# A recurrent attention kernel with a routed feed-forward: another order in the first step and in the tail

## The chip, the cores and the metric

The kernel runs on one core of one Trainium2 chip. The metric is the device time of one execution in microseconds (us). Three executions of the kernel before took 1936.31, 1943.81 and 1943.49 us: the median is 1943.49 us.

## The reference

Two blocks read the same normalised rows `xn` of x (2048 rows of 1024, bf16), and their results are added to x.

```
xn = layernorm(x)
# A: 64 segments of 32 rows, one after the other; mem is 8 rows of 1024
for s in range(64):
    h = concat(mem, xn[32*s : 32*s+32])              # 40 rows
    q, k, v = h @ Wq, h @ Wk, h @ Wv                 # 1024 -> 32 heads x 128
    p = softmax(mask(q k^T * scale))
    o = (p v) @ Wo                                   # 4096 -> 1024
    mem = o[:8]
    out_A[32*s : 32*s+32] = o[8:]
# B: the two rows with the largest xn @ w_r go through a feed-forward of 3584
y = (silu(x_sel @ w_gate) * (x_sel @ w_up)) @ w_down * sigmoid(r_sel)
result = x + out_A + (xn with y added at the two rows)
```

`mem` makes block A a chain of 64 steps. A step's stationary operand holds 32 columns: the 8 memory rows and 24 of the segment's 32 rows. The other 8 rows of each segment, here called the left rows, don't depend on `mem`, and their q, k and v are made for all 64 segments at once in the first step; their attention is done in each step, and their product with Wo again for all segments after the last one.

## The kernel before

**Tiling.** The four weight matrices are cut into 64 granules of 512 KB: granules 0 to 47 are the q, k and v weights in the six phases `PHASES` (q and k of the first half of the heads, q and k of the second half, v of the first half, v of the second half, eight granules each), granules 48 to 63 are Wo. Most stay in SBUF (`resident`). Eighteen (`streamed`) don't fit and are loaded again in each of the 64 steps, from a packed copy `wsc` in DRAM, through five slots (`wstream`). `fetch` issues the next streamed load on SyncE (SP) whenever `after` or `left_done` reports that one has been used. SP issues in program order, so a load that waits for a slot holds all SP loads behind it.

**Step s.** For each phase TensorE multiplies the step's 32 stationary columns by eight granules into PSUM (line 678); hooks between granules do the transposes, scores, softmax (`scores`, `exponent`, `soften`) and `attend`. Then 16 Wo granules are multiplied (`project`, line 712), the result becomes the rows of the output and the memory rows of the next step. `attend` places its sums in PSUM: in the tile WO of pool `psA`, which has two buffers, and in `OPB` for the first half of the heads, in `BS` and `OPB` for the second.

**The first step** does more. It loads all weights, takes the statistics of all 16 tiles of 128 rows (`row_stats`), runs the router (`spread`, `router_tile`, `router_out`, `router_top`), and projects the left rows of all segments: `left_qk` makes 16 heads of q or k, each a chain of eight matmuls into a `psA` buffer and a copy by ScalarE, and stores them to `ql_d` on GpSimd's queue; `left_v` makes 16 blocks of v in the same way, copied in turn by ScalarE and VectorE into four quarters of one SBUF tile VG and stored to `vl_d` on GpSimd's queue (line 496), each quarter being overwritten four blocks later. At the end of `left_v` the rows that step 0 itself needs are read back (tile VL, line 500). `left_done(p)` follows phase p: slots are refilled, and resident areas that served as scratch are loaded (W8B, eight granules, after phase 3; W2 and the last resident granule after phase 5). Before all that come `left_stats` and `left_turns`, which normalise and transpose the left rows.

**The tail** after step 63: `left_rows_out(k)`, k = 0 and 1, multiplies the attention output of the left rows (tile OTA, loaded back from `ol_d` in 16 pieces of 256 KB by `load_left_out`) with the 16 Wo granules (tile WD, line 786; 128 matmuls each), adds x and stores. `gate_up` multiplies the two selected rows by the feed-forward weights (GU, line 848), then come the activation and the product with w_down (YP, line 871). The feed-forward weights are 46 loads (`fetch_moe`), 16 of w_gate and 16 of w_up of 448 KB and 14 of w_down of 512 KB, each needing a home: 22 homes come free during the last step, the others as `gate_up` uses what it has. At the very end the two routed rows are read back from the output, added to and stored.

Of the kernel before, what the change touches and what calls it, by code (L numbers as in the profile page):

```python
# [9 lines left out]
F32 = mybir.dt.float32  # L10
# [18 lines left out]
def kernel(  # L29
# [186 lines left out]
    def left_rows():  # L216
        for t in range(4):
            nc.sync.dma_start(out=XLR[:, t, :], in_=x_left[t, :, XM:SEG, :])

# [208 lines left out]


    left_rows()  # L430
    load_x(0)
    nc.sync.dma_start(out=WRB, in_=B_w_r.unsqueeze(0).to_broadcast([P, D]))
# [24 lines left out]
    left_turns()  # L457
    for t in range(1, NT):
        row_stats(xt(t), S6, MV[:, t, :])

    gathered = {}

    def left_qk(p, mat, half, Gs, between):
        if mat == 0:
            gathered[half] = area(f"big{half}", [P, NSEG, 256], "GA")
        GA = gathered[half].rearrange("p s (m i q r) -> p s m i q r", m=2, i=4, q=4)
        for h in range(16):
            PSG = psA.tile([P, 512], F32, tag="acc", name="PSG")
            for kc in range(KC):
                nc.tensor.matmul(PSG[:, :], lhsT=part(Gs[kc], h // 4)[:, P * (h % 4):P * (h % 4 + 1)], rhs=XLT[:, kc, :],  # L470
                                 start=(kc == 0), stop=(kc == KC - 1))
            nc.scalar.copy(out=GA[:, :, mat, h % 4, h // 4, :], in_=PSG.rearrange("p (s r) -> p s r", r=XL))
            if h % 2 == 1:
                next(between, None)
        for _ in between:
            pass
        if mat == 1:
            G3 = gathered[half]
            if half == 0:
                qkl[0] = one.tile([P, 2, 2, 4, 4, XL], BF16, tag="bA", name="QKL")  # L480
            nc.vector.tensor_copy(out=qkl[0][:, half].rearrange("p m i q r -> p (m i q r)"), in_=G3[:, 0, :])
            for k in range(NSEG // 4):
                nc.gpsimd.dma_start(out=ql_d[k // 2][half, 4 * (k % 2):4 * (k % 2) + 4].rearrange("s p c -> p s c"),
                                    in_=G3[:, 4 * k:4 * (k + 1), :])

    def left_v(half, Gs):
        VG = home(hm, [P, 2048], BF16, "VG")
        for b in range(4):
            for jq in range(4):
                PSV = psA.tile([P, 512], F32, tag="acc", name="PSV")  # L490
                for kc in range(KC):
                    nc.tensor.matmul(PSV[:, :], lhsT=XLT[:, kc, P * b:P * (b + 1)], rhs=part(Gs[kc], jq),  # L492
                                     start=(kc == 0), stop=(kc == KC - 1))
                VQ = VG[:, 512 * jq:512 * (jq + 1)]
                (nc.vector.tensor_copy if jq % 2 else nc.scalar.copy)(out=VQ, in_=PSV[:, :])
                nc.gpsimd.dma_start(out=vl_d[b][4 * jq:4 * jq + 4, :, :, half, :].rearrange("i s r e -> (s r) i e"),
                                    in_=VQ.rearrange("p (i e) -> p i e", i=4))
# [34 lines left out]
    def after(s, g):  # L532
# [17 lines left out]

    def load_left_out(k):
        nc.gpsimd.dma_start(out=areas["big0"][:, 4 * k:4 * k + 4, :], in_=ol_d[k // 4][4 * (k % 4):4 * (k % 4) + 4].rearrange("s p c -> p s c"))

    qkl = [None]
    group = {}

    for s in range(NSEG):
# [113 lines left out]
        for p, (mat, half) in enumerate(PHASES):  # L671
# [13 lines left out]
            if mat < 2:  # L685
# [4 lines left out]
                if s == 0:  # L690
                    left_qk(p, mat, half, [Gv_ for _, Gv_ in behind],
                            (x for g_, Gv_ in behind if g_ in KEPT_COLS for x in keep(g_, Gv_)))
            else:
# [25 lines left out]
        for w in range(16):  # L719
# [60 lines left out]
    def left_rows_out(k):  # L780
        WD = [[psK.tile([P, 512], F32, name=f"WD{2 * b + c}", tag=f"kept{2 * b + c}") for c in range(2)] for b in range(2)]
        for i, (g, Gv) in enumerate(WOS.items()):
            for hs in range(2):
                for b in range(2):
                    for c in range(2):
                        nc.tensor.matmul(WD[b][c][:, :], lhsT=OTR[:, P * (2 * k + b):P * (2 * k + b + 1), 2 * (g - 48) + hs],  # L786
                                         rhs=Gv[:, D * hs + 512 * c:D * hs + 512 * (c + 1)],
                                         start=(i + hs == 0), stop=(i == 15 and hs == 1))
        for b in range(2):
            x = left_x(2 * k + b)  # L790
# [50 lines left out]

    def gate_up(w):
        for kc in range(KC):
            for fh in range(2):
                Gt = moe_tiles["gu", w, kc, fh]
                for fl in range(FC // 2):
                    col = (w * FC + fh * (FC // 2) + fl) * 2
                    nc.tensor.matmul(GU[:, col:col + 2], lhsT=Gt[:, fl * P:(fl + 1) * P], rhs=XSELT[:, kc, :],
                                     start=(w + kc + fh + fl == 0), stop=True, skip_group_check=True)
                free_homes.append(moe_home["gu", w, kc, fh])  # L850
                fetch_moe()

    gate_up(0)
    left_rows_out(1)
    nc.vector.memset(ROW, 0.0)
    for c in range(2):
        nc.gpsimd.dma_start(out=quarters(c), in_=routed(vals[c]))
    gate_up(1)
    assert not moe
# [53 lines left out]
```

## Time and profile before

| | |
|---|---|
| median of three executions | 1943.49 us |
| profiled execution, time | 1954.35 us |
| profiled execution, span of the core | 1952.7 us |
| granted TensorE clock, mean | 0.972 |
| TensorE matmul busy | 1578.2 us (81%) |
| VectorE, ScalarE, GpSimd busy | 907.6, 767.1 and 359.2 us |
| moved by DMA | 672.39 MB, mean 344 GB/s |

A page and several views were taken from one profiled execution. The chain of waits follows the work that ended last back to the start. A timeline row has the start, the duration, the engine and line, output and input tiles, the count of merged instructions, and in brackets the idle time of the engine before them with what ended it. In a table of windows each engine has its busy time and count, then come the granted TensorE clock, the DMA engines' busy share and GB/s.

### The profile page before, as it was taken

What the parts mean: (1) busy time and instruction counts of PE and PEld (TensorE: products, weight loads), DVE (VectorE), ACT (ScalarE), POOL (GpSimd) and SP (SyncE); (2) the same over time, 40 slices, a digit from 0 to 9 for tenths busy, and PEclk for the clock granted to TensorE, in tenths of its full rate; (3) what the DMA queues carried; (4) which work ended last, traced back from release to release, by engine and by line L of the source; (5) the groups of instructions that cost most, each with busy time, mean ns of one, the idle gap of its engine ahead of it and who ended that gap; (6) DMA issues with size and microseconds to landing.
All of it is one profiled execution on the core that took longest, in us unless ns stands there. A gap on an engine that the chain in (4) does not pass through costs nothing.

```text
span 1952.7 us, 70934 instructions
## 1 busy us (share of the span) xinstructions
PE 1578.2 (81%) x30353; PEld 819.4 (42%) x30378; DVE 907.6 (46%) x2774; ACT 767.1 (39%) x2018; POOL 359.2 (18%) x635
## 2 busy tenths in 40 slices
PE   6997678888888888888887888888888888887677
PEld 3443234444444444444443444444444444444345
DVE  7711144555555555555454445545555554454230
ACT  2331134444444444444444444444444444444200
POOL 1224221111111111111111111111111111111300
PEclk9998999999999999999999999999999999999888
DMA  9688299999999999999999999999999999999984
GB/s 351 243 283 258 55 348 369 376 382 366 362 378 369 371 362 367 367 372 371 365 374 344 357 363 375 373 357 353 372 375 365 375 379 365 356 374 355 363 311 172
DMA packets 213853, 672.39 MB, mean 344 GB/s; under 512 B 31424, under 2 KB 34800, under 8 KB 213536
## 3 DMA queue, kind: packets, MB, share of 16 engines
q1 hardware_dynamic: 186896, 617.17, 84.2%
q0 software_dynamic: 25488, 48.58, 7.7%
q8 instruction: 237, 3.88, 0.7%
q10 hardware_dynamic: 1152, 2.10, 0.4%
q14 instruction: 80, 0.66, 0.1%
HBM read 646.74 MB, written 29.76 MB: 346 GB/s over the span
## 4 chain that ended last, share of the span: by engine, by line
DMA 58%; PE 32%; DVE 3%; ACT 3%; issue 2%; POOL 0%; ACTq 0%; SPq 0%; DVEq 0%; POOLq 0%
DMA g<-wsc 54%; PE PSm L678 11%; PE WO L712 7%; PE PSG L470 6%; PE PSV L492 3%; PE WD L786 2%; DMA MW<-in_B_w_gate_dram 1%; PE BT L568 1%; DMA XLS<-in_A_x_dram 1%; ACT OTL L648 1%; ACT OT L646 1%; PE BS L637 1%; DMA MW<-in_B_w_down_dram 0%; DVE BS L601 0%; ACT BS L605 0%
## 5 line engine op out<-in xcount | busy, mean ns | idle before, releaser
L678 PE MATMUL PSm<-wres,ST 128*32 128x512 bf16 x6400 | 539.6, 386 | 22.2 <-DVE ST L333 22.2
L678 PEld LDWEIGHTS <-ST 128*32 128x32 bf16 x12288 | 303.0, 96 | 508.5 <-issue 179.4
L678 PE MATMUL PSm<-g,ST 128*32 128x512 bf16 x3332 | 335.4, 388 | 157.7 <-DMA g<-wsc 153.4
L687 ACT CAST XB<-PSm 128x512 bf16<-128x512 f32 x256 | 150.2, 587 | 265.9 <-PE PSm L678 263.4
L712 PEld LDWEIGHTS <-OT 128*32 128x32 bf16 x8192 | 205.2, 97 | 72.4 <-issue 57.3
L544 POOL DMA_DIRECT2D QKL<-ql_d x63 | 46.9, 744 | 910.7 <-DVE OTL L648 902.7
L578 DVE COPY KT<-BT 128x512 bf16<-128x512 bf16 x128 | 53.1, 415 | 260.8 <-PE BT L568 258.3
L712 PE MATMUL WO<-W8B,OT 128*32 128x256 bf16 x4096 | 164.1, 278 | 0.0
L678 PE MATMUL PSm<-W8A,ST 128*32 128x512 bf16 x2048 | 159.3, 383 | 0.0
L712 PE MATMUL WO<-g,OT 128*32 128x256 bf16 x2560 | 133.1, 279 | 24.2 <-DMA g<-wsc 23.6
L744 POOL DMA_DIRECT2D out_dram<-XN x256 | 128.6, 513 | 84.3 <-DVE XN L742 67.9
L377 ACT COPY BK<-KEPT 128x512 bf16<-128x512 bf16 x126 | 78.3, 621 | 99.0 <-PE WO L712 99.0
L390 DVE COPY g<-KEPT 128x512 bf16<-128x512 bf16 x126 | 53.6, 425 | 134.5 <-PE PSm L678 126.3
L695 ACT CAST VM<-PSm 128x512 bf16<-128x512 f32 x128 | 80.0, 625 | 77.0 <-PE PSm L678 77.0
L573 ACT COPY QT<-BT 128x512 bf16<-128x512 bf16 x128 | 75.0, 586 | 86.1 <-PE BT L568 48.5
L568 PEld LDWEIGHTS <-XB 128*128 128x128 bf16 x1024 | 58.5, 98 | 109.0 <-ACT XB L687 41.5
L568 PE MATMUL BT<-IDENT,XB 128*128 128x128 bf16 x1024 | 102.6, 223 | 0.1
L470 PE MATMUL PSG<-XLT,wres 128*128 128x512 bf16 x324 | 98.7, 379 | 0.3
L595 DVE TENSOR_TENSOR BS<-BS,CT 128x96 f32<-128x96 f32 (+1 forms) x256 | 59.7, 233 | 83.9 <-PE BS L588 79.4
L610 DVE TENSOR_REDUCE DN<-BS 128x8 f32<-128x320 f32 x128 | 62.9, 492 | 67.9 <-ACT BS L605 67.9
L576 ACT COPY KT<-QKL 128x128 bf16<-128x128 bf16 x128 | 38.2, 298 | 138.7 <-PE BT L568 95.5
L294 POOL DMA_DIRECT2D XN<-in_A_x_dram x64 | 34.0, 530 | 301.7 <-PE PSm L678 257.9
(178 smaller groups left out, 2491.8 us busy)
## 6 DMA issues: line engine op xcount, KB each, us to landing
g<-wsc SPq DMA_DIRECT2D x950, 512.0 KB, 6.3
g<-wsc SPq DMA_DIRECT2D x126, 256.0 KB, 5.6
g<-wsc SPq DMA_DIRECT2D x63, 384.0 KB, 5.7
ql_d<-GA POOLq DMA_DIRECT2D x32, 256.0 KB, 6.5
QKL<-ql_d POOLq DMA_DIRECT2D x63, 128.0 KB, 5.5
MW<-in_B_w_gate_dram SPq DMA_DIRECT2D x16, 448.0 KB, 12.7
MW<-in_B_w_up_dram SPq DMA_DIRECT2D x16, 448.0 KB, 9.3
MW<-in_B_w_down_dram SPq DMA_DIRECT2D x14, 512.0 KB, 9.8
```

Of the source, the lines that this page charges most:

```text
L377: copy(out=back[c], in_=KEPT_COLS[KEPT_WHOLE][c])
L470: nc.tensor.matmul(PSG[:, :], lhsT=part(Gs[kc], h // 4)[:, P * (h % 4):P * (h % 4 + 1)], rhs=XLT[:, kc, :], start=(kc == 0), stop=(kc == K ...
L492: nc.tensor.matmul(PSV[:, :], lhsT=XLT[:, kc, P * b:P * (b + 1)], rhs=part(Gs[kc], jq), start=(kc == 0), stop=(kc == KC - 1))
L568: nc.tensor.transpose(out=PTq[:, il, :, :].rearrange("p j r -> p (j r)"), in_=XB[:, il * P:(il + 1) * P], identity=IDENT[:, :])
L573: nc.scalar.copy(out=QT[half][:, :, :], in_=pv)
L595: nc.vector.tensor_tensor(out=S4, in0=S4, in1=m, op=ALU.add)
L610: nc.vector.tensor_reduce(out=DN[:, :], in_=S8, axis=AX.X, op=ALU.add)
L678: nc.tensor.matmul(PSm[32 * jq:32 * jq + 32, :], lhsT=ST[:, kc, :], rhs=part(Gv, jq), start=(kc == 0), stop=(kc == KC - 1), tile_position= ...
L687: nc.scalar.copy(out=XB[:, :], in_=PSm[:, :])
L695: nc.scalar.copy(out=VM[half][:, :], in_=PSm[:, :])
L712: nc.tensor.matmul(PS[32 * g:32 * g + 32, 0:256], lhsT=lhs(h), rhs=Gv[:, D * hs + 256 * g:D * hs + 256 * (g + 1)], start=False, stop=(last ...
L744: nc.gpsimd.dma_start(out=out2[s * SEG:s * SEG + XM, 256 * g:256 * (g + 1)], in_=OB[32 * g:32 * g + XM, :])
```

## The change

In the first step:

- The left rows are loaded on two queues, and ahead of all else come the first column halves of the eight granules of phase 0 (alternately on SP's and ScalarE's queue); x and the second column halves follow.
- The left rows are normalised and transposed first, and `left_qk` makes eight of the 16 heads of phase 0 before `spread`, the normalisation of step 0's rows and the statistics of the other 15 tiles. The other eight heads come after phase 0 as before.
- `left_v` stores on SP's queue, and reads VL back after its second block row instead of after the last.
- W8B is loaded after phase 4 instead of phase 3.
- In step 0 `attend` puts the first half's sums into `BS`, and the `psA` buffer of WO is taken only after all six phases.

In the tail:

- During the last step's Wo product one feed-forward load is issued after each of the five streamed granules, instead of two after each granule.
- Of the 16 loads of OTA, eight are issued on GpSimd's queue in the last step and eight on SP's after the loop, instead of twelve and four on GpSimd's.
- `left_rows_out` finishes its first 128 rows before it begins the second.
- `gate_up` is cut at `early` pieces (22, as 46 loads less 22 homes are left) instead of after w_gate's 16.

```diff
 def left_rows():
     for t in range(4):
-        nc.sync.dma_start(out=XLR[:, t, :], in_=x_left[t, :, XM:SEG, :])
+        (nc.scalar if t % 2 else nc.sync).dma_start(out=XLR[:, t, :], in_=x_left[t, :, XM:SEG, :])
...
+first_phase = []
+def first_half(c):
+    for g, t in first_phase:
+        (nc.scalar if g % 2 and c == 0 else nc.sync).dma_start(
+            out=t[:, D * c:D * (c + 1)], in_=granule_dram(g)[:, D * c:D * (c + 1)])
 left_rows()
+for g in range(KC):
+    ...
+    first_phase.append((g, t))
+first_half(0)
 load_x(0)
...
-for g in range(32):
+first_half(1)
+nc.sync.dma_start(out=WRB, in_=B_w_r.unsqueeze(0).to_broadcast([P, D]))
+for g in range(KC, 32):
...
-left_stats()
-row_stats(xt(0), S6, MV[:, 0, :])
-spread(0, 1)
-norm_seg(0)
-ST = new_st(0)
-mem_to_st(OB, ST)
-left_turns()
-for t in range(1, NT):
-    row_stats(xt(t), S6, MV[:, t, :])
...
-def left_qk(p, mat, half, Gs, between):
+def left_qk(mat, half, Gs, between, h0=0, h1=16):
...
-            nc.gpsimd.dma_start(out=vl_d[b][4 * jq:4 * jq + 4, :, :, half, :].rearrange("i s r e -> (s r) i e"),
-                                in_=VQ.rearrange("p (i e) -> p i e", i=4))
-    if half == 0:
-        group["vl"] = one.tile([P, 2, P], BF16, tag="vl", name="VL")
-    nc.gpsimd.dma_start(out=group["vl"][:, half, :], in_=vl_d[0][:, 0, :, half, :])
+            nc.sync.dma_start(out=vl_d[b][4 * jq:4 * jq + 4, :, :, half, :].rearrange("i s r e -> (s r) i e"),
+                              in_=VQ.rearrange("p (i e) -> p i e", i=4))
+        if b == 1:
+            if half == 0:
+                group["vl"] = one.tile([P, 2, P], BF16, tag="vl", name="VL")
+            nc.sync.dma_start(out=group["vl"][:, half, :], in_=vl_d[0][:, 0, :, half, :])
 def left_done(p):
...
     elif p == 3:
         home_first()
+    elif p == 4:
         area("big1", [P, 8, 2048], "W8B")
         for g in AREAS["big1"]:
             load_resident(g)
 def after(s, g):
...
-        if g >= 47:
-            fetch_moe(2)
+        if g in streamed and g >= 48:
+            fetch_moe(1)
...
+left_stats()
+left_turns()
+row_stats(xt(0), S6, MV[:, 0, :])
+left_qk(0, 0, [t for _, t in first_phase], iter(()), 0, 8)
+spread(0, 1)
+norm_seg(0)
+ST = new_st(0)
+mem_to_st(OB, ST)
+for t in range(1, NT):
+    row_stats(xt(t), S6, MV[:, t, :])
 for s in range(NSEG):
...
-                nxt["wo"] = psA.tile([P, 512], F32, tag="acc", name="WO")
+                if s > 0:
+                    nxt["wo"] = psA.tile([P, 512], F32, tag="acc", name="WO")
...
-            sums[half] = [BS[:, 0:4 * NK] if half else nxt["wo"][:, 256:256 + 4 * NK], OPB]
+            sums[half] = [BS[:, 0:4 * NK] if half or s == 0 else nxt["wo"][:, 256:256 + 4 * NK], OPB]
...
     assert not hooks, hooks
+    if s == 0:
+        nxt["wo"] = psA.tile([P, 512], F32, tag="acc", name="WO")
...
         if w == 2 and s + 1 == NSEG:
-            for k in range(12):
-                load_left_out(k)
+            for k in range(8):
+                load_left_out(k, nc.gpsimd)
...
 fetch_moe()
-for k in range(12, 16):
-    load_left_out(k)
+for k in range(8, 16):
+    load_left_out(k, nc.sync)
...
 def left_rows_out(k):
-    for i, (g, Gv) in enumerate(WOS.items()):
-        for hs in range(2):
-            for b in range(2):
+    for b in range(2):
+        for i, (g, Gv) in enumerate(WOS.items()):
+            for hs in range(2):
                 for c in range(2):
                     nc.tensor.matmul(WD[b][c][:, :], ...)
-    for b in range(2):
         x = left_x(2 * k + b)
...
+pieces = [(w, kc, fh) for w in range(2) for kc in range(KC) for fh in range(2)]
+def gate_up(i0, i1):
+    for w, kc, fh in pieces[i0:i1]:
...
-gate_up(0)
+early = len(pieces) + FC // 2 - len(moe)
+gate_up(0, early)
 left_rows_out(1)
...
-gate_up(1)
+gate_up(early, len(pieces))
```

More of the change, by code (lines that the diff above doesn't have):

```diff
@@ L427, in granule @@
         return t
-    left_rows()
+    first_phase = []
[3 more added lines that the diff above has]
+                out=t[:, D * c:D * (c + 1)], in_=granule_dram(g)[:, D * c:D * (c + 1)])
+    left_rows()
+    for g in range(KC):
+        if g in first_streamed:
+            assert flow.pop(0) == (0, g)
+            t = wstream.tile([P, 2048], BF16, tag="g", name="g")
+            queued.append((g, t))
+        else:
+            t = res_tiles[g] = room(g, f"wres{g}")
+        first_phase.append((g, t))
+    first_half(0)
     load_x(0)
-    nc.sync.dma_start(out=WRB, in_=B_w_r.unsqueeze(0).to_broadcast([P, D]))
     load_seg(0)
@@ L449 @@
         load_resident(g)
[L451 to L459 removed]
     gathered = {}
[L463 to L464 removed]
+    def left_qk(mat, half, Gs, between, h0=0, h1=16):
+        if mat == 0 and h0 == 0:
             gathered[half] = area(f"big{half}", [P, NSEG, 256], "GA")
         GA = gathered[half].rearrange("p s (m i q r) -> p s m i q r", m=2, i=4, q=4)
[L467 removed]
+        for h in range(h0, h1):
             PSG = psA.tile([P, 512], F32, tag="acc", name="PSG")
@@ L549, in load_vl, with load_left_out @@
         nc.gpsimd.dma_start(out=group["vl"][:, :, :], in_=vl_d[s // 16][:, s % 16, :, :, :])
-    def load_left_out(k):
-        nc.gpsimd.dma_start(out=areas["big0"][:, 4 * k:4 * k + 4, :], in_=ol_d[k // 4][4 * (k % 4):4 * (k % 4) + 4].rearrange("s p c -> p s c"))
+    def load_left_out(k, queue):
+        queue.dma_start(out=areas["big0"][:, 4 * k:4 * k + 4, :], in_=ol_d[k // 4][4 * (k % 4):4 * (k % 4) + 4].rearrange("s p c -> p s c"))
     qkl = [None]
     group = {}
+    left_stats()
[8 more added lines that the diff above has]
+        row_stats(xt(t), S6, MV[:, t, :])
     for s in range(NSEG):
@@ L690 @@
                 if s == 0:
-                    left_qk(p, mat, half, [Gv_ for _, Gv_ in behind],
-                            (x for g_, Gv_ in behind if g_ in KEPT_COLS for x in keep(g_, Gv_)))
+                    left_qk(mat, half, [Gv_ for _, Gv_ in behind],
+                            (x for g_, Gv_ in behind if g_ in KEPT_COLS for x in keep(g_, Gv_)), 0 if p else 8)
             else:
@@ L840 @@
     GU = psA.tile([P, 512], F32, tag="acc", name="GU")
[L842 to L851, printed above, removed]
-    gate_up(0)
+    pieces = [(w, kc, fh) for w in range(2) for kc in range(KC) for fh in range(2)]
+    def gate_up(i0, i1):
+        for w, kc, fh in pieces[i0:i1]:
+            Gt = moe_tiles["gu", w, kc, fh]
+            for fl in range(FC // 2):
+                col = (w * FC + fh * (FC // 2) + fl) * 2
+                nc.tensor.matmul(GU[:, col:col + 2], lhsT=Gt[:, fl * P:(fl + 1) * P], rhs=XSELT[:, kc, :],
+                                 start=(w + kc + fh + fl == 0), stop=True, skip_group_check=True)
+            free_homes.append(moe_home["gu", w, kc, fh])
+            fetch_moe()
+    early = len(pieces) + FC // 2 - len(moe)
+    gate_up(0, early)
     left_rows_out(1)
```

## The prediction

> **What bounds the kernel now.** I read the table of windows over the three stages first, then the chain of waits.
>
> ```profile
> core 0: us, PE busy (x) PEld busy (x) DVE busy (x) ACT busy (x) POOL busy (x), PEclk, DMA share, GB/s
> 0.00:259.00 259.00, 204.35 (x1330) 95.52 (x1353) 95.57 (x213) 66.37 (x124) 68.57 (x113) 0.95 0.70 241
> 259.00:1829.00 1570.00, 1287.04 (x28056) 666.85 (x28044) 791.35 (x2505) 693.88 (x1878) 276.47 (x502) 0.99 0.99 368
> 1829.00:1952.00 123.00, 86.81 (x982) 57.02 (x981) 20.73 (x58) 6.83 (x16) 14.20 (x22) 0.79 0.74 265
> ```
>
> The middle, 1570 us, is the steps' weight stream: the DMA share is 0.99, and the change touches none of its transfers, so I carry it over unchanged. The ends are different: 0.30 x 259 = 78 us of the DMA engines stand unused in the first step and 0.26 x 123 = 32 us in the tail. What shortens those two stages moves the end, as the bytes fit into less time.
>
> In the first step the second half has the holes. On TensorE's timeline and the SP queue's:
>
> ```profile
> 152.28 0.39 PE L492 MATMUL PSV<-W8A,XLT 128*128 128x512 bf16 x1
> 173.03 1.01 PE L492 MATMUL PSV<-W8A,XLT 128*128 128x512 bf16 x2 [10.22 <-ACT VG L495]
> 192.39 0.38 PE L492 MATMUL PSV<-W8A,XLT 128*128 128x512 bf16 x1
> 197.84 0.24 PE L637 MATMUL WO<-PT,VL 32*128 32x160 bf16 x1 [3.87 <-DMA VL<-vl_d]
> 200.73 0.58 PE L492 MATMUL PSV<-W8A,XLT 128*128 128x512 bf16 x1 [0.72 <-ACT VM L695]
> 243.39 0.38 PE L492 MATMUL PSV<-wres,XLT 128*128 128x512 bf16 x1
> 251.48 0.31 PE L637 MATMUL BS<-PT,VL 32*128 32x160 bf16 x1 [6.38 <-DMA VL<-vl_d]
> 251.99 17.15 SPq L354 DMA_DIRECT2D g<-wsc  x14
> ```
>
> These give the first `left_v` (152.3 to 192.8), its wait for VL, the second `left_v` (200.7 to 243.8), its wait for VL, and the start of the stream at 252. GpSimd's and ScalarE's timelines tell why:
>
> ```profile
> 160.45 5.95 POOL L483 DMA_DIRECT2D ql_d<-GA  x8 [3.73 <-issue]
> 166.39 2.97 POOL L496 DMA_DIRECT2D vl_d<-VG  x4
> 187.67 0.59 ACT L495 CAST VG<-PSV 128x512 bf16<-128x512 f32 x1 [2.87 <-PE PSV L492]
> 191.13 0.59 ACT L495 CAST VG<-PSV 128x512 bf16<-128x512 f32 x1 [2.87 <-PE PSV L492]
> 209.61 0.59 ACT L495 CAST VG<-PSV 128x512 bf16<-128x512 f32 x1 [4.64 <-PE PSV L492]
> 214.88 0.59 ACT L495 CAST VG<-PSV 128x512 bf16<-128x512 f32 x1 [4.69 <-PE PSV L492]
> ```
>
> The first four v stores stood behind sixteen ql_d stores on GpSimd's queue, and their quarters of VG could not be overwritten. ScalarE copies every second block: 3.46 us for two blocks, 1.73 each, is the pace with two PSUM buffers; 5.27 for two, 2.64 each, that of the second `left_v`, where WO holds one buffer and the copy stands between the chains.
>
> **The first step, part by part.** *Start.*
>
> ```profile
> 11.34 1.92 DVE L227 TENSOR_SCALAR XLR<-XLR,MISC 128x1024 bf16<-128x1024 bf16 x4
> 15.18 0.24 PE L254 MATMUL BT<-MISC 128*128 128x2 bf16 x4 [15.18 <-ACT MISC L246]
> 18.88 0.19 DVE L333 COPY ST<-BT 128x64 bf16<-128x64 bf16 x1 [1.34 <-PE BT L309]
> 20.52 1.02 ACT XLT L235
> 22.59 2.62 PE PSm L678 x32
> 26.43 1.29 DVE L241 BATCH_NORM_STATS2 MISC<-XP 128x6 f32<-128x512 bf16 x2
> 28.00 1.29 DVE L241 BATCH_NORM_STATS2 MISC<-XP 128x6 f32<-128x512 bf16 x2
> 55.08 0.27 PE BT L254 x4
> ```
>
> The left rows are normalised at 13.3 as before; four turns, two in flight, each with a copy of up to 1.02, end near 17.0. Eight heads at 1.73 take TensorE to 30.9. Then ScalarE's last copy and the square root (0.8), and the chain from `spread` to the stationary tile, 15.18 to 19.07 = 3.9, in which TensorE has next to nothing. Phase 0 starts at 35.7 and takes 2.6, the other eight heads 13.8 and the kept pieces' transposes about 2: 54.2, hardly earlier than the 55.08 of before. The earlier start is eaten by the hole of 4.7 us, and a new wait comes behind. The 15 tiles' statistics are queued on VectorE behind the stationary copy, which now waits for eight heads: they run from 35.8 at 1.57 each, to 59.4, and the second `spread`, which TensorE must pass before phase 1, comes at 59.9 instead of 55.08, **4.8 us later**. The router's work, behind it on VectorE, moves with it.
>
> The 4 to 5 us hole and the one before 59.9 also cool TensorE:
>
> ```profile
> 160.00:180.00 20.00, 9.56 (x35) 3.90 (x34) 1.48 (x3) 1.17 (x2) 11.18 (x16) 0.74 0.94 278
> 175.97 1.49 PE L492 MATMUL PSV<-W8A,XLT 128*128 128x512 bf16 x3
> 177.25 0.63 PE L492 MATMUL PSV<-g,XLT 128*128 128x512 bf16 x1
> ```
>
> After the hole at 162.8 the granted clock of that window is 0.74, and three matmuls stand at 0.43 us each, twice the 1.73/8 = 0.216 of the pace; from 173.03 to beyond 177.25 is some 4.3 us at half pace, which costs about 2. The first hole's cost is covered by VectorE's statistics; for the second I add 1. **Start: +5.8**, bounds -1 (the statistics hidden after all) and +8 (both holes paid). The Trainium skill, "TensorE: Matmul & The Clock Gate", Part 1, says that an idle window of about 3.4 us halves the array's clock until a busy window of that length has passed, which speaks against this part; by that rule both holes are paid, with about 1.7 us each, and the sum would be 1 to 2 us worse. The row at 0.43 us agrees.
>
> *First `left_v`.* 40.5 us fall to 16 x 1.73 = 27.7: **-12.8**. SP has nothing ahead of them but the four issues of `left_done(3)`, since W8B is moved. SP storing 256-byte pieces is not in this trace. Nearest is GpSimd's own:
>
> ```profile
> L496 POOL DMA_DIRECT2D vl_d<-VG x32: 750/750/764, 166.4 to 244.8; - x32
> DMA to landing us min/median/max: 2.4/2.6/6.5
> ```
>
> A quarter of VG is overwritten 6.9 us after its copy, plus one PSUM buffer's 1.7: landing times of 2.4 to 6.5 both fit, so I take zero, bounds 0 and +6 (two such landings of 6.5 in a row, against 6.9).
>
> *First wait for VL.* Its read-back is now behind the eighth store, 14 us earlier. But `attend` writes BS, which `soften(1)` reads:
>
> ```profile
> 194.51 0.21 DVE L617 TENSOR_TENSOR PL<-BS,DN 128x64 bf16<-128x64 f32 x1
> ```
>
> VectorE is done with BS at 194.72, 0.75 after TensorE stood ready at 193.97; behind that matmul stands all of TensorE. 3.87 become 0.75: **-3.1**.
>
> *Second `left_v`.* Both PSUM buffers are free: 43.0 to 27.7. W8B (eight loads) and two slot refills now lie on SP ahead of these stores, and the refills can go only when the first `left_v` has ended. Their 5.2 MB at 368 GB/s take 14 us, until about when the fifth block wants its quarter (5.1 us of phase 5, then 5 x 1.73); I take 1.5 us of waiting: **-13.8**, bounds -15.3 and 0 (rival B).
>
> *Second wait for VL.* The 6.38 us go; the stream's first load comes next on SP, behind the last store's landing, and its bytes behind 2.6 MB (two refills, W2, the last resident granule), 7 us at that rate. Before, 8.2 us lay between the end of `left_v` and the first stream load, with the engines mostly idle, and the load of the last resident granule went with it: **-2**, bounds 0 and -6.4.
>
> First step: 5.8 - 12.8 - 3.1 - 13.8 - 2.0 = **-25.9 us**.
>
> **The tail.**
>
> ```profile
> 1826.38 5.97 POOL L552 DMA_DIRECT2D OTA<-ol_d  x8 [12.58 <-DMA g<-wsc]
> 1847.64 16.53 PE L786 MATMUL WD<-W8B,OTA 128*128 128x512 bf16 x61 [7.18 <-DMA OTA<-ol_d]
> 1873.90 8.92 DMA g<-wsc
> 1882.86 3.62 PE L786 MATMUL WD<-g,OTA 128*128 128x512 bf16 x16 [2.43 <-DMA g<-wsc]
> 1890.83 6.10 PE L848 MATMUL GU<-T,MW 128*128 128x2 bf16 x224
> 1899.83 16.24 PE L786 MATMUL WD<-W8B,OTA 128*128 128x512 bf16 x62 [2.89 <-issue]
> 1929.27 2.48 DVE L793 TENSOR_TENSOR XLS<-XLS,WD 128x512 bf16<-128x512 bf16 x4 [38.17 <-PE WD L786]
> 1940.22 0.60 POOL L857 DMA_DIRECT2D T<-out_dram  x1 [81.31 <-DMA out_dram<-XLS]
> ```
>
> The first WD ends at 1886.4, because the last Wo granule lay on SP behind 22 feed-forward loads and landed at 1882.8. Now four lie ahead of it: with five granules 2.6 + 1.8 MB of SP's, OTA's and x's 3.1 MB beside them and 1.5 MB (three granules) in flight, 9.0 MB or 24.5 us at 368 GB/s from 1830: 1855. WD's first 128 rows can start near 1840 (before, it was the second 128 that waited until 1847.64): 64 matmuls to 1857, paced by the landings, and 64 x 0.216 = 13.8 for the second, cover for the x rows' normalisation: 1870.8, **-15.6**. Then 4.4 us of small operations less 1.2 (half the additions, 2.48/2, are done), and 22 pieces of `gate_up` at 6.10/16 = 0.38, 8.4 us: the second WD starts at 1882.4 instead of 1899.8. Its first OTA pieces are there: the 9.0 MB, 18 more loads (8.3) and OTA's next megabyte make 18.4 MB, 50 us from 1829: 1879. WD runs warm, 27.7, to 1910.1. The remaining feed-forward loads but two run beneath it. Behind it the chain is the addition (1.2 less), the store, the read-back of line 857 and the last addition: 23.4 us from 1929.3 to the span's end before, 22.2 now. End at 1932.3: **-20.4 us**, bounds -10 (landings of OTA on SP) and -25.
>
> Sum: -25.9 - 20.4 = **-46.3 us**, from the profiled execution's 1954.35 (span 1952.7) to 1908.0. That execution lies 10.9 us above the median of the runs shown, so I say **1897 us**.
>
> **The rivals.** *B, the stores behind W8B.* SP's queue delivers in order, and the second `left_v` runs at the pace of landings, 2.6 us each: 16 x 2.6 = 41.6, as slow as before. 13.8 us of the gain go: 1911. For it: ten large loads ahead; against: they are over when the fifth block comes. *C, the tail pays half.* OTA's 256 KB pieces on SP behind 17 loads come at the spacing of before (eight issued from 1826.4, there at 1847.6, 2.65 each, 21 us), and the second WD waits some 10 us: 1907. *D, slower.* If 256-byte stores on SP's queue cost the queue itself, each `left_v` runs at their pace; the point is 1.73 us each, and at 1.73 + 46/32 = 3.2 all the gain is gone. At the longest landing above, 6.5, one after another, 32 x (6.5 - 1.73) = 153 us are lost from the forecast: 2050. Against: GpSimd issues one in 0.75, and landings overlap. *E, the queue was not the cause.* If the DMA engines, at 0.94 share between 160 and 180, held the first v stores, the hole of 10.2 and its cold 2 stay: 1909. For it: that share; against: the stores were not issued before 166.39. The Trainium skill, "DMA: Bandwidth & Descriptors", section "Issuing engines are not separate DMA queues", says that another issuing engine saves only the sequencer's time to issue, usually small, since all run on the same 16 engines; by that rule E is what happens. The trace here has the issue itself late by 11 us. *F, nothing:* a wait unseen gives it all back: 1943.
>
> **How the numbers follow.** Forecast 0.63, B 0.10, C 0.10, E 0.07, D 0.06, F 0.04. Low end: start -1, -15.3 for the second `left_v`, -6.4 for its VL and -25 in the tail give -64: 1880. High end: start +8 with B and C together gives -20: 1923; with B and the first `left_v` 6 us short it is 1919. What is left out is D, F and the outer ends. A measurement of this kernel can tell about 0.5%, 10 us, from no change. Faster by more: A, B, C, E but for a little: 0.90; within: 0.04; slower: 0.06.
>
> **What would show it.** Right: `spread` near 60 with VectorE's statistics just before it; no hole in the first `left_v`, 1.73 us per block in both; the stream's first load near 226; the second WD near 50 us after the last Wo product began; the middle still near 1570 us. Wrong: SP rows of line 496 that follow one another at more than 1.73 us, copies that wait for vl_d, or a middle stage that grows.

## The result, and the profile after

The changed kernel took 1923.74 us (median of 11 executions, 1912.2 to 1934.65); the kernel before, run beside it, 1946.28 us (median of 11, 1936.31 to 1955.12). The ratio is 0.988, with a 95% interval of 0.9849 to 0.9911: faster by 23 us (17 to 29). The forecast was 1897 us, in a range of 1880 to 1923: the direction was right, the size was half of what was forecast, and the time lies 0.7 us above the upper end of the range. The profiled execution after took 1924.64 us, span 1923.0, against 1954.35 and 1952.7 before.

The table of windows over the three stages, after:

```profile
core 0: us, PE busy (x) PEld busy (x) DVE busy (x) ACT busy (x) POOL busy (x), PEclk, DMA share, GB/s
0.00:249.00 249.00, 205.06 (x1331) 95.83 (x1353) 95.32 (x213) 66.48 (x124) 44.31 (x80) 0.95 0.74 254
249.00:1819.70 1570.70, 1288.48 (x28060) 669.34 (x28053) 791.30 (x2505) 695.65 (x1882) 276.73 (x501) 0.99 0.98 367
1819.70:1923.00 103.30, 81.23 (x971) 56.24 (x976) 20.66 (x58) 6.32 (x14) 8.03 (x14) 0.88 0.89 315
```

The tail fell from 123.1 to 103.3 us and its DMA share rose from 0.74 to 0.89. The first step fell only by some 10 us; its DMA share went from 0.70 to 0.74. TensorE's timeline of the first step, after (start, duration, engine and line, output and input, count, idle time before it and what ended it):

```profile
61.84 0.27 PE L254 MATMUL BT<-MISC 128*128 128x30 bf16 x4 [5.23 <-ACT MISC L246]
...
160.33 0.39 PE L499 MATMUL PSV<-W8A,XLT 128*128 128x512 bf16 x1
...
172.15 0.59 PE L499 MATMUL PSV<-W8A,XLT 128*128 128x512 bf16 x2 [1.29 <-ACT VG L502]
...
182.75 0.59 PE L499 MATMUL PSV<-W8A,XLT 128*128 128x512 bf16 x2 [3.54 <-ACT VG L502]
...
192.89 0.38 PE L499 MATMUL PSV<-W8A,XLT 128*128 128x512 bf16 x1
195.28 0.22 PE L658 MATMUL BS<-PT,VL 32*128 32x160 bf16 x1 [0.81 <-DVE PL L637]
197.26 0.38 PE L499 MATMUL PSV<-W8A,XLT 128*128 128x512 bf16 x1 [0.16 <-issue]
...
213.15 1.01 PE L499 MATMUL PSV<-W8A,XLT 128*128 128x512 bf16 x2 [5.58 <-ACT VG L502]
...
232.91 0.38 PE L499 MATMUL PSV<-wres,XLT 128*128 128x512 bf16 x1
239.12 0.62 PE L735 MATMUL WO<-g,OT 128*32 128x256 bf16 x8 [2.09 <-DMA g<-in_A_Wo_dram]
242.54 0.62 PE L735 MATMUL WO<-W,OT 128*32 128x256 bf16 x8 [2.80 <-DMA W<-in_A_Wo_dram]
244.35 0.62 PE L735 MATMUL WO<-W,OT 128*32 128x256 bf16 x8 [1.20 <-DMA W<-in_A_Wo_dram]
```

The second `spread` is late, the first `left_v` has two holes and the second one, and a new wait for Wo's loads stands where the wait for VL was. The holes are those of the copies, which waited for quarters of VG. ScalarE and the SP queue, after:

```profile
171.51 0.59 ACT L502 CAST VG<-PSV 128x512 bf16<-128x512 f32 x1 [5.21 <-DMA vl_d<-VG]
182.12 0.59 ACT L502 CAST VG<-PSV 128x512 bf16<-128x512 f32 x1 [7.41 <-DMA vl_d<-VG]
212.51 0.59 ACT L502 CAST VG<-PSV 128x512 bf16<-128x512 f32 x1 [9.50 <-DMA vl_d<-VG]
...
162.93 16.93 SPq L503 DMA_DIRECT2D vl_d<-VG  x8
182.73 11.66 SPq L503 DMA_DIRECT2D vl_d<-VG  x8
195.77 6.37 SPq L138 DMA_DIRECT2D W8B<-in_A_Wo_dram  x8
202.72 17.88 SPq L503 DMA_DIRECT2D vl_d<-VG  x8
238.41 2.48 SPq L354 DMA_DIRECT2D g<-wsc  x4
```

The same 128 KB store landed at very different times. The view of tile VG, cut to the stores issued at 162 to 170, 170 to 176, 180 to 194, 200 to 208 and 221 to 235 us, in this order:

```profile
DMA to landing us min/median/max: 7.2/7.8/8.5
DMA to landing us min/median/max: 8.2/9.7/9.9
DMA to landing us min/median/max: 1.9/2.0/3.9
DMA to landing us min/median/max: 7.5/8.1/8.8
DMA to landing us min/median/max: 1.9/1.9/2.0
```

Alone a store lands in 2 us (DMA share 0.44 between 180 and 194, 0.34 between 221 and 235). It took 7 to 10 while GpSimd's sixteen `ql_d` stores were running (DMA share 0.99 between 160 and 180), and 8 behind W8B's eight loads. These are copies that wait for vl_d, one of the signs of being wrong that were named ahead. The tail, after (TensorE, then SP):

```profile
1857.97 4.48 PE L809 MATMUL WD<-g,OTA 128*128 128x512 bf16 x20
1866.08 6.10 PE L871 MATMUL GU<-T,MW 128*128 128x2 bf16 x226
1874.10 2.35 PE L871 MATMUL GU<-T,MW 128*128 128x2 bf16 x82 [1.93 <-issue]
1876.82 8.91 PE L809 MATMUL WD<-W8B,OTA 128*128 128x512 bf16 x31 [0.37 <-issue]
1906.29 3.64 PE L871 MATMUL GU<-T,MW 128*128 128x2 bf16 x140
1912.14 4.65 PE L895 MATMUL YP<-MW,T 128*2 128x256 bf16 x112 [2.21 <-DVE YP L889]
...
1866.04 9.21 SPq L561 DMA_DIRECT2D OTA<-ol_d  x8
1883.34 24.35 SPq L418 DMA_DIRECT2D MW<-in_B_w_down_dram  x14
```

The first WD ends at 1862.4 and the second begins at 1876.8, 57.1 us after the last Wo product began at 1819.7.

### The profile page after: what moved, and what is told of

It is laid out like the page before. It is cut to its first block, busy times and chain, and to the rows that moved or that the text cites. A ratio compares the mean times of both kernels' runs of the same rounds, so it can differ in the third digit from the quotient of the medians.

```text
span 1923.0 us, 70950 instructions
## 1 busy us (share of the span) xinstructions
PE 1574.8 (82%) x30354; PEld 821.4 (43%) x30378; DVE 907.3 (47%) x2774; ACT 768.4 (40%) x2018; POOL 329.1 (17%) x593
## 5 line engine op out<-in xcount | busy, mean ns | idle before, releaser
L699 PE MATMUL PSm<-g,ST 128*32 128x512 bf16 x3332 | 338.4, 391 | 163.5 <-DMA g<-wsc 159.7
```

The costliest lines, as they stand in the source:

```text
L699: nc.tensor.matmul(PSm[32 * jq:32 * jq + 32, :], lhsT=ST[:, kc, :], rhs=part(Gv, jq), start=(kc == 0), stop=(kc == KC - 1), tile_position= ...
```

## The experiments

All of them are read at the same marks, taken from each kernel's timelines in us of its span: the second `spread`, the length of each `left_v`, the end of step 0, which is VectorE's first cast of the Wo sums to XN (before: 257.11, after: 246.39), and the tail, counted from the start of the last step's Wo product to the end of the span. "Middle" is what lies between the last two marks.

| kernel | 2nd spread | first left_v: start, length | second left_v: length | step 0 ends | middle | tail |
|---|---|---|---|---|---|---|
| before | 55.1 | 152.3, 40.5 | 43.0 | 257.1 | 1572.5 | 123.1 |
| after | 61.8 | 160.3, 32.9 | 36.0 | 246.4 | 1573.3 | 103.3 |
| old start (1) | 55.0 | 152.2, 32.6 | 33.5 | 235.3 | 1567.7 | 103.0 |
| q, k stores paced (2) | 62.3 | 161.0, 27.8 | 38.0 | 244.2 | 1568.7 | 105.4 |
| W8B spread (3) | 60.7 | 159.5, 33.7 | 27.6 | 238.8 | 1556.3 | 103.2 |
| v on GpSimd (4) | 62.7 | 161.5, 39.7 | 28.6 | 253.2 | 1562.4 | 102.1 |
| before + PSUM part (5) | 54.1 | 151.3, 39.8 | 29.3 | 241.9 | 1560.5 | 124.5 |
| before + tail (6) | 55.2 | 152.4, 40.4 | 43.0 | 257.2 | 1555.7 | 105.1 |
| 1 + 2 + 3 together (7) | 54.7 | 151.9, 27.8 | 27.6 | 225.3 | 1569.1 | 105.2 |
| 2 + 3, new start (8) | 62.4 | 161.2, 27.8 | 27.6 | 234.4 | 1567.1 | 103.2 |
| 8 + spread later (9) | 62.7 | 159.1, 27.8 | 27.6 | 232.0 | 1561.1 | 105.1 |
| before + start (10) | 62.4 | 161.1, 39.8 | 43.0 | 265.2 | 1566.5 | 122.9 |

The marks of one part agree within about 2 us wherever that part is the same (the first `left_v` of the six kernels with the new start begins at 159.5 to 161.5, kernel 9 aside). The middle does not: the kernel before and the one with only its tail changed issue the same work up to the last step, and their middles are 1572.5 and 1555.7. So a part is judged by its mark, and by the time only where several executions were taken.

**1. The old start.** The changed kernel with the loads, the statistics and `left_qk` in the order of before:

```diff
...
 left_stats()
-left_turns()
 row_stats(xt(0), S6, MV[:, 0, :])
-left_qk(0, 0, [t for _, t in first_phase], iter(()), 0, 8)
 spread(0, 1)
...
+left_turns()
 for t in range(1, NT):
...
```

> The changed kernel with the start of the kernel before: loads, statistics and transposes in the old order, all 16 heads of phase 0 after it. Theory (the new start costs, by the statistics queued behind the stationary copy): the first left_v begins near 152 us of the span as before the change, not 160; everything after it moves by 8 us, and the time falls by 6 to 9 us from the changed kernel's. Rival (the new order only shows up late, and the 8 us come from something after phase 0): the first left_v still begins near 160 and the time stays.

The first `left_v` begins at 152.19, 8.1 us earlier, step 0 ends 11.1 earlier, and the time was 1902.21 us (4 executions), ratio 0.9781 (0.9721 to 0.9841). The new order of the start is a loss. Of the 3 us by which step 0 moved further than the 8 expected, 2.5 lie in the second `left_v` (33.5 instead of 36.0); why is not shown. The ratio is further from the changed kernel's 0.988 than 8 to 11 us (0.4 to 0.6%) would make it; the two were timed in different sessions, and the intervals leave room for that.

**2. The q and k stores out of the way.** The sixteen `ql_d` stores of the second half are issued one for each block of the first `left_v`, after that block's copy:

```diff
...
+                if half == 0:
+                    nc.gpsimd.tensor_copy(out=PACE[:, :], in_=VQ[:, 0:4])
+                    store_ql(1, 4 * b + jq)
...
```

> The changed kernel, but the 16 ql_d stores of the second half of the heads are issued on GpSimd one at a time, each after one more block of the first left_v has been copied, instead of all at once. Theory (the v stores wait on DMA engines that the ql_d stores keep full): v stores land in 2 to 4 us, the two holes of the first left_v go, it takes 28 to 29 us instead of 32.9, and the first step ends 4 us sooner. Rival (a store in 256-byte pieces on SP's queue is slow by itself): the holes stay, 32 to 34 us.

TensorE's first and last rows of the first `left_v` in this kernel:

```profile
160.95 0.39 PE L504 MATMUL PSV<-W8A,XLT 128*128 128x512 bf16 x1
188.37 0.38 PE L504 MATMUL PSV<-W8A,XLT 128*128 128x512 bf16 x1
```

27.8 us without a hole: 16 blocks of 1.73, the length forecast. So SP can carry these stores, and what held them was the traffic beside them. The stores landed in 2.5 us at the median, at most 4.3. The second `left_v`, whose W8B was still ahead of its stores, took 38.0, 2 us more than in the changed kernel, and step 0 ended only 2.2 earlier, where 4 were expected.

**3. W8B spread.** Its eight loads are issued one after every second store of the second `left_v`, instead of all ahead of it:

```diff
+                if half == 1 and jq % 2 == 0:
+                    load_resident(AREAS["big1"][2 * b + jq // 2])
...
         area("big1", [P, 8, 2048], "W8B")
-        for g in AREAS["big1"]:
-            load_resident(g)
```

> The changed kernel, but the eight W8B loads are issued on SP one after every second block of the second left_v, instead of all eight ahead of it. Theory (the v stores stand behind W8B on SP's own queue): the second left_v takes 28 to 30 us instead of 36.0, its hole of 5.6 goes. Rival (store pieces slow by themselves): 35 to 37 us, the hole only moves.

The second `left_v` took 27.6 us, with no hole, and step 0 ended 7.6 earlier. The one execution took 1899.94 us, but 17 us of its gain on the changed kernel lie in the middle and are not to be credited to this edit.

**4. The v stores back on GpSimd's queue**, and VL read back at the end:

```diff
-            nc.sync.dma_start(out=vl_d[b][4 * jq:4 * jq + 4, :, :, half, :]...
+            nc.gpsimd.dma_start(out=vl_d[b][4 * jq:4 * jq + 4, :, :, half, :]...
...
```

> The changed kernel with the v stores and both read-backs of VL on GpSimd's queue as before the change. Theory (queue order on GpSimd made the first hole, the DMA engines only a part of it): the first left_v takes 39 to 41 us again instead of 32.9, and the wait for VL is back with 3 to 4 us; the second left_v, with two PSUM buffers and W8B on another queue, 28 to 32 us, then 6 us of wait for VL. Rival (the issuing queue makes no difference, only the DMA engines do): the first left_v stays at 32 to 34.

GpSimd's and ScalarE's rows in this kernel:

```profile
168.87 5.95 POOL L490 DMA_DIRECT2D ql_d<-GA  x8 [2.89 <-issue]
174.81 2.97 POOL L503 DMA_DIRECT2D vl_d<-VG  x4
181.00 0.58 ACT L502 CAST VG<-PSV 128x512 bf16<-128x512 f32 x1 [13.48 <-DMA vl_d<-VG]
208.78 0.31 PE L657 MATMUL BS<-PT,VL 32*128 32x160 bf16 x1 [6.30 <-DMA VL<-vl_d]
```

The first `left_v` is back at 39.7 us: the first v store, of a quarter whose copy began at 163.5, is issued at 174.81 behind the last `ql_d` store. The move to SP is therefore worth 39.7 - 32.9 = 6.8 us, and the `ql_d` traffic takes the other 32.9 - 27.8 = 5.1; the traffic was not moved with the v stores still on GpSimd, so the shares hold for this order of the two steps. The wait for VL is back too, with 6.30 us where 3 to 4 were expected. The second `left_v` is fast here, 28.6, with GpSimd's queue free and W8B alone on SP; its first store was issued at 215.1, 8 us after the issue of the last W8B load, so this run doesn't tell whether stores on another queue would have landed sooner beside those loads.

**5. The PSUM part alone**, in the kernel before:

```diff
-                nxt["wo"] = psA.tile([P, 512], F32, tag="acc", name="WO")
+                if s > 0:
+                    nxt["wo"] = psA.tile([P, 512], F32, tag="acc", name="WO")
...
-    sums[half] = [BS[:, 0:4 * NK] if half else nxt["wo"][:, 256:256 + 4 * NK], OPB]
+    sums[half] = [BS[:, 0:4 * NK] if half or s == 0 else nxt["wo"][:, 256:256 + 4 * NK], OPB]
...
+        if s == 0:
+            nxt["wo"] = psA.tile([P, 512], F32, tag="acc", name="WO")
```

> The kernel before with one part of the change: in step 0 the first half's sums go to BS, and WO takes its PSUM buffer after all six phases. Theory (one PSUM buffer made the second left_v's 2.64 us a block): it takes 28 to 30 us instead of 43, the wait for VL stays at 6 to 8 us, the first step ends 13 to 15 us sooner. Rival (the stores on GpSimd's queue, or their landing, set that pace too): 36 us or more.

The second `left_v` fell from 43.0 to 29.3 us by this alone; step 0 ended 15.2 earlier than before, 4.5 us more than the whole change brought it. So the -13.8 of the forecast was there to be had, and the move of W8B and of the stores took half of it back.

**6. The tail alone**, in the kernel before: the issue of one feed-forward load after each streamed Wo granule, OTA's loads in eights, the first 128 rows finished first, and the cut at 22 pieces.

```diff
-        if g >= 47:
-            fetch_moe(2)
+        if g in streamed and g >= 48:
+            fetch_moe(1)
...
```

> The kernel before with the tail of the change alone. Theory (the two ends add up): the stage from the last Wo product to the end takes 103 us instead of 123, the time falls by 18 to 22 us. Rival (the tail's gain needs the first step's): less than 15.

The tail was 105.1 us instead of 123.1, and the time 1927.60 us (10 executions) against 1945.47 (17), ratio 0.9903 (0.9867 to 0.9940): 19 us (12 to 26). By the mark, 18.0 us, the tail stands by itself; the interval of the time alone would leave room for the rival's 15.

**7. Both obstacles and the start undone together**, edits 1, 2 and 3 in the changed kernel.

> The changed kernel with the old start, the paced ql_d stores and the spread W8B loads together. Theory (start, ql_d stores and W8B are three separate causes): 8 + 4 + 6 = 18 us less than the changed kernel, about 1906. Rival (one wait takes the place of another, such as the Wo loads behind the second left_v, 6.4 us there already): 8 to 11 us less.

TensorE's first and last rows of the two `left_v` in this kernel:

```profile
151.92 0.39 PE L487 MATMUL PSV<-W8A,XLT 128*128 128x512 bf16 x1
179.34 0.38 PE L487 MATMUL PSV<-W8A,XLT 128*128 128x512 bf16 x1
...
183.77 0.38 PE L487 MATMUL PSV<-W8A,XLT 128*128 128x512 bf16 x1 [0.16 <-issue]
210.96 0.38 PE L487 MATMUL PSV<-wres,XLT 128*128 128x512 bf16 x1
```

Step 0 ends at 225.25, 21.1 us earlier than in the changed kernel. The three edits alone moved it by 11.1, 2.2 and 7.6, together 20.9, so by this mark the three causes add up; 18 were expected. It is 31.9 us earlier than before, and the time is 1901.54 us (6 executions) against 1945.47, ratio 0.9769 (0.9717 to 0.9821). This is the fastest version by its ratio, faster than the kernel before and, by intervals that don't meet, than the changed kernel; from kernel 1 its time can't be told apart.

**8 and 9. The price of the start.** Kernel 8 is kernel 7 with the new start; kernel 9 issues the second `spread` and the router's tiles after phase 1's eighth granule instead of before its first:

```diff
-            spread(1, NT)
-            for t in range(NT):
-                router_tile(t)
...
+            hook(1, 7, router_rows)
```

> The changed kernel with its own start, but with the second half's q and k stores spread over the first left_v and W8B's loads spread over the second, so that neither holds the v stores. Theory (the new start is a loss of its own, of about 8 us, whatever comes behind it): the second spread near 62, the first left_v begins near 160.5 instead of the 151.9 of the version with the old start, both left_v take 27.7, step 0's result is cast near 233.5 instead of 225.25, and the median is about 8 us over that version's 1901.5: 1909. Rival (the start's 8 us are taken back by waits further on, since the transfers of the first step set its end): the cast comes near 226 and the median near 1902.

> The same kernel with one edit more: the second spread and the 16 router tiles behind it are issued after phase 1's eighth granule instead of before its first, about 4.3 us later for TensorE. Theory (the start's loss is TensorE waiting for 15 tiles' statistics on VectorE): TensorE reaches the second spread near 60.9 and the statistics end at 61.4 as before, so the hole of 5.2 us falls to about 1 and the cold matmuls behind it go; the first left_v begins near 154 and step 0's result is cast near 227, 6 to 7 us ahead of the kernel without this edit; median near 1903. Rival (the loads in another order and the cold array are the loss): the first left_v still begins near 159 to 160 and the cast stays near 232.

The second `spread` in kernel 8, and in kernel 9:

```profile
62.38 0.27 PE L255 MATMUL BT<-MISC 128*128 128x30 bf16 x4 [5.25 <-ACT MISC L247]
```

```profile
62.74 0.25 PE L255 MATMUL BT<-MISC 128*128 128x30 bf16 x4 [2.97 <-ACT MISC L247]
```

Kernel 8 ends step 0 at 234.35, 9.1 us behind kernel 7, and its time is 1906.36 us against 1940.5, ratio 0.9839 (0.9793 to 0.9885). The loss isn't taken back later; in time the two intervals overlap. For kernel 9 my number was wrong: phase 1 fills the hole with 2.6 us, the length the prediction used for phase 0, and not with the 4.3 I wrote. The hole shrank by 2.3 and the first `left_v` began 2.0 earlier, at 159.14; that and the cast at 232.04 are the rival's figures. The hole of 2.97 that is left still ends with VectorE's statistics, as in kernel 8, so the run doesn't speak against them, but it gave back only 2.3 of the 9 us. Kernels 1, 8 and 10 show that the start as a whole is the loss; that the statistics set its end is read from the traces, and no run here separates them from the other order of the loads. Kernel 9's time, 1908.13 us, ratio 0.9842 (0.9799 to 0.9884), is not to be told from kernel 8's.

**10. The start alone**, in the kernel before.

> The kernel before with the new start alone (left rows first, the loads in the new order, eight heads ahead of the first spread); v is stored by GpSimd, W8B is loaded after phase 3, WO holds a PSUM buffer in step 0 and the tail is as before. Theory (the new start costs 8 us and nothing else changes): the second spread near 62, the first left_v begins near 160.3, step 0's result is cast near 265 instead of 257.1, the stage of the weight stream stays within its spread of 1556 to 1573 us, and the time is 8 us over the kernel before: ratio 1.004. Rival (the new start also lengthens the weight stream, since the three kernels with it gained 7 to 12 us less in time than their two ends gave): the cast near 265 too, but 15 to 20 us in time, ratio 1.008 to 1.010.

The row of the second `spread` and VectorE's cast at the end of step 0 in this kernel:

```profile
62.41 0.27 PE L254 MATMUL BT<-MISC 128*128 128x30 bf16 x4 [5.25 <-ACT MISC L246]
265.24 0.42 DVE L760 CAST XN<-WO 128x256 bf16<-128x256 f32 x1 [1.68 <-PE WO L730]
```

Step 0 ends 8.1 us later, and the time is 1951.06 us (12 executions) against 1941.93 (17), ratio 1.0055 (1.0032 to 1.0078): 11 us slower (6 to 15). The middle, 1566.5, is within its spread. The start's own loss is shown by mark and time; whether it also makes the weight stream a few us longer, the interval doesn't settle.

## Why the prediction was half right

The forecast of the parts was -25.9 us for the first step and -20.4 for the tail. By the marks it was 246.39 - 257.11 = -10.7 and 103.3 - 123.1 = -19.8, with the middle 0.8 longer: -29.7 in the profiled spans. What failed is the first step.

**Start: forecast +5.8, bounds -1 and +8; measured +8.0.** The mechanism is the one described: VectorE's 15 statistics stand behind the stationary copy, and TensorE idles 5.23 us before the second `spread`, where it idled about 1 before. The first matmul of the eight heads, the first of the 15 statistics, and the square root that releases the `spread`, after:

```profile
17.97 0.59 PE L477 MATMUL PSG<-XLT,wres 128*128 128x512 bf16 x1 [1.10 <-ACT XLT L235]
37.65 1.27 DVE L241 BATCH_NORM_STATS2 MISC<-XP 128x6 f32<-128x512 bf16 x2
61.57 0.22 ACT L246 ACTIVATE MISC<-MISC 128x15 bf16<-128x15 bf16 x1 [4.56 <-DVE MISC L245]
```

Of the 8.0, 4.2 are this longer hole, 2.5 a later arrival of TensorE at it (56.6 instead of 54.1) and 1.3 the cold matmuls behind it (granted clock 0.62 between 62 and 66): the first `left_v` comes 98.5 us after the `spread`, before it was 97.2. The forecast had the `spread` at 59.9, and it came 1.9 later, because the statistics began at 37.65 and not at 35.8. The step that was mis-sized is the eight heads: they began at 17.97 instead of 17.0 and took 15.3 us instead of 13.8, as their first matmuls followed one another at 0.43 us. The cold matmuls behind the `spread` cost 1.3 where I had put 1. So the upper bound was the right value, but by luck: it was set for the cold matmuls behind both holes. Phase 0 did take 3.5 us behind the first hole (37.8 to 41.3, granted clock 0.60 between 38 and 42) instead of 2.6, but the statistics ran beneath it, and it cost nothing, as the forecast said. The rule of the Trainium skill cited there ("TensorE: Matmul & The Clock Gate", Part 1) agrees with the half pace behind both holes; that the sum came out 2.2 worse, near its 1 to 2, is no proof of the price, since only the second hole was paid.

**First `left_v`: forecast -12.8, measured -7.6.** The step that failed is the landing time. I took 2.4 to 6.5 us from GpSimd's stores, found them under the 8.6 us that four quarters and two PSUM buffers give, and set the waiting to zero. Those rows came from stores that had waited until the `ql_d` traffic had been issued; on SP the first stores run beside it, and landed in 7.8 and 9.7 at the median. Kernel 2 shows the forecast 27.8 as soon as that traffic is moved. The bound of +6 held (5.2 measured). **Rival E**, that the DMA engines and not the queue held the stores, was posed as one or the other, and it is both: 6.8 us of the 12 were the queue's order (kernel 4), 5.1 the traffic beside the stores (kernel 2). The rule of the Trainium skill on which E leaned ("DMA: Bandwidth & Descriptors", "Issuing engines are not separate DMA queues") calls the time to issue, the one thing that another issuing engine saves, usually small. Here it was the larger part: the v stores' issue fell from 11 us late, behind sixteen other issues, to at once, and that alone was worth 6.8.

**First wait for VL: forecast -3.1, measured -4.0.** TensorE now waits 0.81 us for VectorE's PL, forecast 0.75.

**Second `left_v`: forecast -13.8, measured -7.0.** Here the 1.5 us of waiting for W8B was mis-sized, and rival B is half true. I reckoned the 5.2 MB over at about the time when the fifth block wants its quarter, and left out the store's own issue and landing behind them and the cold matmuls after the hole. The eight loads were issued from 195.77 to 202.14, and the first store only at 202.72, although its quarter had been copied at 199.6; then the first stores took 8.1 us to land at the median. TensorE stood 5.58 us, and ran cold after it (two matmuls in 1.01 at 213.15, granted clock 0.77 between 206 and 221), which makes up the other 2.8 of the 8.4 us over the 27.6 of kernel 3. What is left of B's story, the pace of landings for all 16 blocks, was not seen: from 221.9 on the stores landed in 1.9. Kernels 3 and 5 remove and bypass the loads, and reach 27.6 and 29.3. How much of the late landing is the queue's order and how much the loads' share of the DMA engines is not separated.

**Second wait for VL: forecast -2.0, measured -0.2.** I named what comes next, the refills, W2 and the last granule, and gave it too small a price. TensorE waits 2.09, 2.80 and 1.20 us for them between 237 and 244. They can't be issued before the last store, since SP is in order, and two of them need slots that `left_v` reads to its end. Kernel 7, with nothing else in the way, takes 13.9 us from the end of `left_v` to the cast, like the 13.3 of before. This wait replaces the one removed. That is read from the traces: no run here moves these loads.

**The tail: forecast -20.4, measured -19.8, but by errors that cancel.** Counted from the last Wo product, the first WD ends 14.1 us earlier (15.6 forecast) and the second begins 13.1 earlier (17.4 forecast), 57.1 us after it and not about 53: the first WD gave 1.5 of these 4.3 us, and `gate_up`'s first part 2.0, which took 10.4 (1866.08 to 1876.45, with a wait of 1.93) instead of 8.4. The second WD took 29.5 us, as before the change, and not the 27.7 of a warm array: its first 6 us, behind that wait and one of 0.37, ran at a granted clock of 0.59. Behind the second WD I had 1.2 us of gain, and it was 6.7, as I had read the chain there as addition, store and read-back. In the kernel before, the chain that ended last went another way: the last eight w_down loads were issued only when the second `gate_up` had begun to free their homes, behind the second WD, and YP stopped for them three times, 2.96 us together. Its rows:

```profile
1929.72 5.96 PE L848 MATMUL GU<-T,MW 128*128 128x2 bf16 x224
1930.24 6.94 SPq L418 DMA_DIRECT2D MW<-in_B_w_down_dram  x8
1943.76 0.39 PE L871 MATMUL YP<-MW,T 128*2 128x256 bf16 x8 [0.95 <-DMA MW<-in_B_w_down_dram]
1945.26 0.39 PE L871 MATMUL YP<-MW,T 128*2 128x256 bf16 x8 [1.11 <-DMA MW<-in_B_w_down_dram]
1946.55 0.60 PE L871 MATMUL YP<-MW,T 128*2 128x256 bf16 x8 [0.90 <-DMA MW<-in_B_w_down_dram]
```

With the cut at 22 pieces all 14 w_down loads were issued between 1883.34 and 1907.7, nearly all beneath the second WD; YP ran in one piece, and the row of `gate_up` fell from 224 to 140 matmuls, 5.96 to 3.64 us. Rival C's wait didn't come: no row of the second WD waits for OTA.

**The other rivals.** D, that 256-byte stores slow SP's queue itself, is refuted by kernel 2: issue 0.36 us each, landing in 2.5 at the median of the first `left_v`. F, that all is given back, is refuted by the result.

**From the sum to the time.** The profile before lay 8 us over its median and the profile after 1, so -29.7 between the profiled executions became -22.5 between the medians (ratio: -23, interval -29 to -17). The difference is of the size by which the middle varies from one execution to the next, 1556 to 1573 us. Kernel 7, in which the v stores land as the forecast had them and the start is the old one, ends step 0 31.9 us earlier and has a tail 17.9 shorter, and its time falls by 45 us (35 to 55): there, what the two ends give does appear in the time. It doesn't in every kernel with free stores: kernels 8 and 9 gained 31 us in time where their ends give 43, the latter beyond the upper end of both intervals (40 and 39); where the rest went is open.

The range failed at its high end, 1923. It took the start at its bound with B and C, but no loss in the first `left_v` and only the forecast in the second wait. What came was a part of each: 2.2 us in the start, 5.2 and 6.8 in the two `left_v`, 1.8 in the second wait, less 0.9 gained in the first. (The 1919 given for B with a first `left_v` 6 us short should be 1917.)

## What to carry to other kernels

Price a store that a buffer waits for by its landing time in the traffic that will run beside it after the move, not by rows from a time when the queue had kept that traffic apart. Where loads are moved to another place in an in-order queue, look at the stores that now lie behind them, and spread the loads between the stores. Work that is queued on a second engine ahead of something TensorE must pass (here 15 statistics) counts from the moment at which that engine is free, and what makes TensorE busy earlier can make that moment later.

## What the runs showed of the hardware

- The same 128 KB store in 256-byte pieces on SP's queue landed in 1.9 to 2.0 us at the median with the DMA engines little used (share 0.34 to 0.44), 7.8 to 9.7 beside sixteen 256 KB stores of another queue (share 0.99), and 8.1 behind eight 512 KB loads on its own. Its issue took 0.36 us on SP where nothing held it, and up to 3.3 beside that traffic; on GpSimd it took 0.75.
- Two profiled executions that issue the same work in the stage of the weight stream (kernels before and 6) differ there by 17 us, 1%, while the marks of the first step agree within 0.3 us. A change of a few us at the ends is seen in marks much sooner than in times.
